# Pooled attention and a tanh-shrink MLP on one core: output stores moved to ScalarE's queue, q cast and turned by token blocks, pair sums one pair sooner

## The chip, the cores and the metric

The kernel runs on one core of a Trainium2 chip. The core has a matrix engine (TensorE, PE in the profile, PEld for its weight loads), VectorE (DVE), ScalarE (ACT), GpSimd (POOL), and SyncE (SP), which here only issues transfers. Transfers run on 16 DMA engines; SyncE and ScalarE each have a queue from which they issue them. The metric is the time of one execution in microseconds (us), lower is better.

## The reference, cut to what matters

Attention over keys and values that are averaged in groups of 8 rows, for 8 batches, 8 heads, 576 tokens and a head size of 64; its output, 4608 tokens by 512, goes through a two-layer MLP with 2048 hidden units.

```python
k_p = k.reshape(B, H, Sp, 8, D).mean(axis=3)          # Sp = 72
v_p = v.reshape(B, H, Sp, 8, D).mean(axis=3)
scores = scale * np.matmul(q, k_p.transpose(0, 1, 3, 2))
attn = np.exp(scores - scores.max(-1, keepdims=True))
attn = attn / (attn.sum(-1, keepdims=True) + 1e-9)
x = np.matmul(attn, v_p).transpose(0, 2, 1, 3).reshape(B * S, H * D)
h = x @ w_in                                           # 512 -> 2048
out = (h - np.tanh(h)) @ w_out                         # 2048 -> 512
```

## The kernel before, in words

The MLP works on groups of 512 tokens, nine of them (`g` = 0 to 8), the attention on batches of 576. Batch `nb = g + 1` is attended to while group `g` is in the MLP, and the inputs of batch `nn = g + 2` are loaded meanwhile. Group 0 has code of its own; the change is in the loop over groups 1 to 8, and "group" below means one turn of it.

A group has two stages. In the first, **h stage**, TensorE makes `h` in eight pairs of hidden blocks (`h_pair`, matmuls on L529, 8 per pair; the last pair as two halves, `h_one`). For each pair ScalarE takes the tanh (L541, L546), and VectorE subtracts it from `h` in PSUM and writes `Gt` in bf16 (L542, L547). `sum_p` (L550) adds the two members of finished pairs into `P`, two pairs in one instruction.

In the second stage the output product is done in seven smaller ones instead of eight, by Strassen's scheme: `product` (L585) multiplies `Gt`, `P`, `Q` or `Dg` with stored sums of the weights, in two halves of four pairs each, and `after_product` combines the seven in SBUF into `O`, which holds four tiles of 128 tokens by 512. The first product reads `Gt`, the second and third `P`. Between the half products TensorE does the scores of the next batch (L348), which need the turned q (`qT`), and, from the seventh on, attention times v (L395), whose result is turned by DMA into `xT` (L433), the next groups' MLP input.

q of the next batch comes from DRAM into `q_raw` (one buffer), is cast to bf16 by ScalarE into `q_bf` (`q_cast_part`, L192: two casts of four heads each, all four token blocks; L197: the 64 tokens left over), and turned by five DMA transposes (`q_dma_transpose`, L203). The three casts are issued before the tanhs of the first three pairs (pairs 1 to 3 in group 1), the five transposes after the last cast. The pooled k is turned likewise (L331) at the first pair. Right after the q transposes SyncE issues the nine loads of batch `nn`: k in two (L137, L146), v in five (L137, four times L141), q in two (L170, L162).

The results are stored by SyncE (`store`, L602): the upper two tiles of `O` (`store(g, 1)`) after the thirteenth half product, the lower two (`store(g, 0)`) at the group's end. Tokens are dealt over partitions in an interleaved order, so that a tile's rows are one or two stretches of the output, each with a transfer of its own.

Each engine's instructions run in the order in which the kernel states them[...]. Between engines the framework puts in the waits, and it deals completion counters to the transfers after a planner has lined up the engines' instructions by estimated time.

Of the kernel before, what the change touches and what calls it, by code (L numbers as in the profile page):

```python
# [9 lines left out]
BF16 = mybir.dt.bfloat16  # L10
# [5 lines left out]
B, H, S, D = 8, 8, 576, 64  # L16
POOL = 8
G = S // POOL
DM, DFF = 512, 2048
NHP = H // 2  # L20
R = 4
# [5 lines left out]
TG = 512  # L27
# [8 lines left out]
HT = TG // 2  # L36
# [6 lines left out]
def kernel(  # L43
# [9 lines left out]
    nc = tc.nc  # L53
# [5 lines left out]
    work = ctx.enter_context(tc.tile_pool(name="work", bufs=2))  # L59
# [44 lines left out]
    O = const.tile([128, 4, DM], FP32, name="O")  # L104
# [9 lines left out]
    q_bf = const.tile([128, R + 1, H, D], BF16, name="q_bf")  # L114
# [35 lines left out]
    def load_k(b):  # L150
        return [
            load_main(k_pairs, k_raw[b % 2], b, 0, NM),
            load_dense(k_pairs, k_raw[b % 2], b),
        ]

    def load_v(b):
        return [load_main(v_pairs, v_raw[b % 2], b, 0, NM)] + load_left(
            v_pairs, v_raw[b % 2], b
        )
# [6 lines left out]
    def load_q(b, tail=True):  # L166
        if b not in q_raws:
            q_raws[b] = raw.tile([128, H, R + 1, D], FP32, name="q_raw", tag="q_raw")
        t = q_raws[b]
        nc.sync.dma_start(  # L170
            out=t[:, :, 0:R, :], in_=q[b, :, 0:QA, :].rearrange("h (p j) d -> p h j d", j=R)
        )
        if tail:
            load_q_tail(b, t, nc.sync)

    qTs = {}
# [12 lines left out]
    def q_cast_part(b, n):  # L189
        t = q_raws[b]  # L190
        if n < 2:
            nc.scalar.copy(  # L192
                out=q_bf[:, 0:R, 4 * n : 4 * n + 4, :].rearrange("p j h d -> p h j d"),
                in_=t[:, 4 * n : 4 * n + 4, 0:R, :],
            )
        else:
            nc.scalar.copy(out=q_bf[:QT, R, :, :], in_=q_raws.pop(b)[:QT, :, R, :])  # L197

    def q_dma_transpose(b):
        qT = work.tile([128, NHP, S], BF16, name="qT", tag="qT")  # L200
        for j in range(R + 1):
            rows = 128 if j < R else QT
            nc.sync.dma_start_transpose(  # L203
                out=qT[:, :, j * 128 : j * 128 + rows],
                in_=q_bf[:rows, j, :, :].rearrange("p h d -> p (h d)"),
            )
        qTs[b] = qT

    def q_pe_transpose(b, hps, eng=None):
        if b not in qTs:  # L210
# [86 lines left out]
    def kb_main(kb, ps, t0, t1, engs):  # L297
        kv = kb.rearrange("p (t x) -> p t x", x=KP)
        engs[0](out=kv[0:D, t0:t1, 0:G], in_=ps[0:D, :, 0:G])
        engs[1](out=kv[D:128, t0:t1, G:128], in_=ps[D:128, :, G:128])  # L300

    def kb_left(kb, ps, eng):
        eng(
            out=kb[D:128, :].rearrange("p (t x) -> p t x", x=KP)[:, :, 128 : 128 + LO],
            in_=ps[D:128, 0 : NM * LO].rearrange("p (x t) -> p t x", t=NM),
        )
# [22 lines left out]
    def k_dma_transpose(b):  # L329
        kT = work.tile([128, NT, 128], BF16, name="kT", tag="kT", bufs=1)  # L330
        nc.sync.dma_start_transpose(  # L331
            out=kT[:, :, :], in_=kdups.pop(b)[:, :, :, :].rearrange("p t a d -> p (t a d)")
        )
        kTs[b] = kT

    def k_place(b, eng):
        kT = kTs.pop(b)
        kb_main(KB[b % 2], kT[:, 0:NM, :], 0, NM, (eng, eng))
        kb_left(KB[b % 2], kT[:, NM, :], eng)
# [115 lines left out]
    def out_segments(c0, nrows):  # L455
        segs = []
        r = 0
        while r < nrows:
            c = c0 + r
            bb = c // S  # L460
            i = c % S
            if i < QA:
                j = i // 128
                p0 = i % 128
                ln = min(128 - p0, nrows - r, QA - i)
                dst = out[bb * S : bb * S + QA, :].rearrange("(p j) m -> p j m", j=R)[
                    p0 : p0 + ln, j, :
                ]
            else:
                ln = min(S - i, nrows - r)  # L470
                dst = out[bb * S + i : bb * S + i + ln, :]
            segs.append((r, r + ln, dst))
            r += ln
        return segs
# [62 lines left out]
    def h_pair(g, p, b0, ts):  # L537
        h_mms(g, p, PS[:, b0, :])
        h_mms(g, p + NP, PS[:, b0 + 1, :])
        t2 = TS[:, 2 * ts : 2 * ts + 2, :]  # L540
        nc.scalar.activation(out=t2, in_=PS[:, b0 : b0 + 2, :], func=ACT.Tanh)  # L541
        nc.vector.tensor_sub(out=Gt[:, p, :, :], in0=PS[:, b0 : b0 + 2, :], in1=t2)  # L542

    def h_one(g, p, s, b0, ts):
        h_mms(g, p + s * NP, PS[:, b0, :])
        nc.scalar.activation(out=TS[:, ts, :], in_=PS[:, b0, :], func=ACT.Tanh)  # L546
        nc.vector.tensor_sub(out=Gt[:, p, s, :], in0=PS[:, b0, :], in1=TS[:, ts, :])  # L547

    def sum_p(a, b):
        nc.vector.tensor_tensor(  # L550
            out=P[:, a:b, :], in0=Gt[:, a:b, 0, :], in1=Gt[:, a:b, 1, :], op=ALU.add
        )

    def sum_q(a, b):
        nc.vector.tensor_tensor(
            out=Q[:, a:b, :], in0=Gt[:, a:b, 0, 0:HT], in1=Gt[:, a:b, 1, HT:TG], op=ALU.add
        )
# [9 lines left out]
    def w_sum(out, a, b, op, eng=nc.vector, k0=0, k1=NP):  # L567
        return eng.tensor_tensor(  # L568
            out=out[:, k0:k1, :], in0=a[:, k0:k1, :], in1=b[:, k0:k1, :], op=op
        )  # L570
# [23 lines left out]
    def chain(g, bk):  # L594
        if g == NG - 1 and bk == C1:
            return PS[:, 2:4, 0:HD]
        return PS[:, bk, :].rearrange("p (t n) -> p t n", t=2)

    def store(g, th, tts=(0, 1), c0=0, c1=DM):
        for tt in tts:  # L600
            for n, (r0, r1, dst) in enumerate(out_segments(g * TG + th * HT + tt * 128, 128)):
                nc.sync.dma_start(out=dst[:, c0:c1], in_=O[r0:r1, 2 * th + tt, c0:c1])  # L602

    def sh(c, off):
        return slice(c.start + off, c.stop + off)
# [99 lines left out]
    for m, base, step, cm in (  # L705
# [6 lines left out]
            out=m,  # L712
            in_=m,
# [6 lines left out]
    for i in range(2):  # L720
# [4 lines left out]
        out=spread.rearrange("p (t x) -> p t x", x=32)[:, :, 0:LO],  # L725
        in_=ident[:, 0 : NM * LO].rearrange("p (x t) -> p t x", t=NM),
# [156 lines left out]
    for u in range(16):  # L883
        qd, tb = u // 4, u % 4
# [27 lines left out]
        if u in (9, 11):  # L912
            n = (u - 9) // 2
            nc.scalar.mul(
                out=w2s[:, 4, 4 * n : 4 * n + 4, :], in_=b22[:, 4 * n : 4 * n + 4, :], mul=-1.0
# [10 lines left out]
    for g in range(1, NG):  # L926
        nb = g + 1 if g + 1 < B else None
        nn = g + 2 if g + 2 < B else None
        for p in range(NP - 1):
            c = p if g > 1 else p - 1  # L930
            if nb is not None and 0 <= c < 3:
                q_cast_part(nb, c)
            h_pair(g, p, (0, 2, 4, 6, 0, 2, 4)[p], p % 2)
            if g == 1 and p < 4:
                w_sum(w2s[:, 0, :, :], b11, b22, ALU.add, k0=2 * p, k1=2 * p + 2)
            if p >= 4:
                sum_p(2 * p - 8, 2 * p - 6)
            if nb is not None and p == 0:
                k_dma_transpose(nb)
                k_place(nb, nc.gpsimd.tensor_copy)  # L940
            if nb is not None and c == 2:
                q_dma_transpose(nb)
                if nn is not None:
                    load_k(nn)
                    load_v(nn)
                    load_q(nn)
        h_one(g, NP - 1, 1, 0, 2)
        h_one(g, NP - 1, 0, 1, 3)
        sum_p(6, 8)
        sum_q(0, 4)  # L950
        sum_q(4, 8)
        ps_a = Banks(2, 3, 4, 5, 0, 1)
        for u in range(14):
            n, half = u // 2, u % 2
            bk, lhs, rhs = products[n]
            if n == 6 and g == NG - 1:
                break
            product(g, bk, lhs, rhs, 4 * half, 4 * half + 4, n < 2)
            if half:
                after_product(g, n)  # L960
                if g == 1 and n in (1, 2):
                    w_sum(w2s[:, 2, :, :], b21, b22, ALU.add, k0=4 * n - 4, k1=4 * n)
            if nb is not None:
                if u < NT:
                    scores(nb, u)
                if u in (6, 7, 8, 9, 11):
                    av(nb, (6, 7, 8, 9, 11).index(u), ps_b1, True)
                if u == 6 and nn is not None:
                    pool_k(nn, nc.gpsimd)
                    pool_v(nn, nc.gpsimd)  # L970
            if u == 12:
                store(g, 1)
        if g < NG - 1:
            nc.scalar.copy(out=O[:, 0:2, 0:HD], in_=chain(g, C1))  # L974
            store(g, 0)
    store(NG - 1, 1)
    store(NG - 1, 0, c0=HD)
    bk, lhs, rhs = products[6]
# [40 lines left out]
```

## Time and profile before

Time before: 308.95 us, the median of 3 runs (308.21 to 310.93). The profiled execution has a span of 306.2 us at a mean granted TensorE clock of 0.989.

| view | what | us |
|---|---|---|
| busy | TensorE matmuls | 282.6 (92%) |
| busy | VectorE | 230.3 (75%) |
| busy | ScalarE | 154.1 (50%) |
| group | L529 h stage, 512 matmuls of 379 ns | 111.8 |
| group | L541 tanh of a pair, 56 of 1024 ns | 57.3 |
| group | L542 subtraction of a pair, 56 of 1221 ns | 68.4 |
| group | L550 pair sums, 32 of 683 ns | 21.8 |
| group | L192 casts of q, 12 of 1042 ns | 12.5 |
| SyncE's queue | L602 stores, 52 of 594 ns (median) | to landing 2.4 |
| SyncE's queue | L203 q transposes, 30 of 1257 ns (median) | to landing 2.5 |

Busy time is what an engine spent on instructions, not what it adds to the end. In the list of waits a line names who waited, for whom, the us in all, how often, and the longest. In a timeline a line gives the start, the length of a run of like instructions, the engine (SPq: SyncE's queue, where the length is that of issuing, not of the transfer), the line of code, and in brackets the idle time before it with what ended it.

### The profile page before, as it was taken

How to read it: one execution, taken by the hardware profiler on the slowest of the kernel's cores; microseconds unless marked ns; L12 is line 12 of the kernel's file. 1: busy time of each engine (PE TensorE's matmuls, PEld its weight loads, DVE VectorE, ACT ScalarE, POOL GpSimd, SP SyncE). 2: the span in 40 equal slices, each digit the busy share in tenths (PEclk: the TensorE clock that was granted, in tenths of full speed). 3: DMA queues.
4: the chain of work that ended last, by engine and by line, in shares of the span. 5: the costliest groups of instructions: out<-in, count | busy, mean ns of one | idle time of the engine just before them, and what ended most of it. 6: DMA issues, size and time to landing. Idle time of an engine off the chain costs nothing.

```text
span 306.2 us, 5451 instructions
## 1 busy us (share of the span) xinstructions
PE 282.6 (92%) x2040; PEld 179.3 (59%) x2040; DVE 230.3 (75%) x400; ACT 154.1 (50%) x244; POOL 121.3 (40%) x122
## 2 busy tenths in 40 slices
PE   7999899998989599999999978999998999999990
PEld 3554356446944388458745863479447945864780
DVE  5658577799968759598869883899687948937960
ACT  4657576676256352765275525660865056136320
POOL 8500819940793019802961296109910100100010
PEclk9999999999999899999999999999999999999997
DMA  7999999939637598749974997499560360040005
GB/s 260 217 222 276 314 243 296 205 77 322 161 62 176 116 334 134 193 77 347 174 167 98 333 157 186 91 323 186 118 146 2 64 153 2 0 131 8 0 9 130
DMA packets 66378, 49.84 MB, mean 163 GB/s; under 512 B 39984, under 2 KB 53296, under 8 KB 66352
## 3 DMA queue, kind: packets, MB, share of 16 engines
q1 hardware_dynamic: 59024, 42.94, 56.8%
q0 software_dynamic: 4752, 4.72, 9.2%
q10 hardware_dynamic: 2576, 1.84, 2.2%
q8 instruction: 16, 0.26, 0.4%
q14 instruction: 10, 0.08, 0.1%
HBM read 36.70 MB, written 9.44 MB: 151 GB/s over the span
## 4 chain that ended last, share of the span: by engine, by line
PE 60%; DMA 15%; DVE 12%; POOL 4%; ACT 3%; issue 3%; SPq 2%; ACTq 0%; POOLq 0%; DVEq 0%
PE PS L585 25%; PE PS L529 23%; DVE Gt L542 6%; DMA w1b<-in_moe_w_in_dram 4%; DMA qT<-q_bf 4%; PE PS L511 4%; DMA k_raw<-in_k_dram 4%; PE PS L348 3%; PE PS L395 3%; DMA xT<-x_sb 3%; DVE P L550 2%; ACT TS L541 2%; DVE w2s L568 1%; POOL k_raw L247 1%; SPq L203 1%
## 5 line engine op out<-in xcount | busy, mean ns | idle before, releaser
L529 PE MATMUL PS<-xT,w1b 128*128 128x512 bf16 x512 | 111.8, 379 | 4.7 <-DMA xT<-x_sb 3.8
L542 DVE TENSOR_TENSOR Gt<-PS,TS 128x1024 bf16<-128x1024 f32 x56 | 68.4, 1221 | 33.2 <-ACT TS L541 33.2
L529 PEld LDWEIGHTS <-w1b 128*128 128x128 f16 x512 | 49.8, 98 | 64.2 <-issue 3.7
L541 ACT ACTIVATE TS<-PS 128x1024 f32<-128x1024 f32 x56 | 57.3, 1024 | 35.0 <-PE PS L529 27.7
L626 POOL TENSOR_TENSOR m<-O,m 128x512 f32<-128x512 f32 x8 | 10.5, 1312 | 127.1 <-ACT m L625 65.5
L413 DVE TENSOR_TENSOR x_sb<-PS,rden 128x256 bf16<-128x256 f32 x72 | 30.5, 424 | 2.5
L585 PE MATMUL PS<-w2s,Dg 128*128 128x256 f16 x256 | 30.2, 273 | 0.0
L585 PEld LDWEIGHTS <-Gt 128*128 128x128 bf16 x256 | 24.8, 99 | 8.8 <-DVE Gt L547 2.7
L367 ACT ACTIVATE E<-PS 128x288 bf16<-128x288 f32 x60 | 21.8, 410 | 13.9 <-PE PS L348 13.7
L247 POOL TENSOR_TENSOR k_raw<-k_raw 128x512 f32<-128x512 f32 (+2 forms) x13 | 21.6, 1679 | 16.8 <-DMA k_raw<-in_k_dram 16.8
L585 PEld LDWEIGHTS <-P 128*128 128x128 bf16 x256 | 24.8, 99 | 5.0 <-issue 1.4
L585 PEld LDWEIGHTS <-Dg 128*128 128x128 bf16 x256 | 24.6, 98 | 2.7
L348 PE MATMUL PS<-qT,KB 128*128 128x288 bf16 (+5 forms) x128 | 18.1, 293 | 5.9 <-DMA qT<-q_bf 5.7
L560 DVE TENSOR_TENSOR Dg<-Gt 128x1024 bf16<-128x1024 bf16 x32 | 22.1, 750 | 0.0
L550 DVE TENSOR_TENSOR P<-Gt 128x1024 bf16<-128x1024 bf16 x32 | 21.8, 683 | 0.3
L395 PE MATMUL PS<-VB,E 128*128 128x130 bf16 x240 | 20.2, 220 | 0.1
L632 ACT COPY m<-PS 128x512 f32<-128x512 f32 x8 | 4.7, 585 | 29.5 <-PE PS L585 29.5
L585 PE MATMUL PS<-w2s,Gt 128*128 128x256 f16 x128 | 18.0, 282 | 1.6 <-DVE Gt L547 1.5
L266 POOL TENSOR_TENSOR v_raw<-v_raw 128x512 f32<-128x512 f32 (+1 forms) x12 | 19.2, 1620 | 0.0
L395 PEld LDWEIGHTS <-E 128*128 128x128 bf16 x240 | 16.8, 98 | 1.9 <-issue 0.4
L585 PE MATMUL PS<-w2b,P 128*128 128x256 f16 x128 | 16.6, 276 | 0.0
L974 ACT COPY O<-PS 128x512 f32<-128x512 f32 x7 | 4.1, 586 | 24.6 <-PE PS L585 24.6
(108 smaller groups left out, 386.0 us busy)
## 6 DMA issues: line engine op xcount, KB each, us to landing
k_raw<-in_k_dram SPq DMA_DIRECT2D x7, 1024.0 KB, 5.8
q_raw<-in_q_dram SPq DMA_DIRECT2D x7, 1024.0 KB, 10.2
v_raw<-in_v_dram SPq DMA_DIRECT2D x7, 1024.0 KB, 8.4
out_dram<-O SPq DMA_DIRECT2D x36, 128.0 KB, 2.4
out_dram<-O SPq DMA_DIRECT2D x16, 256.0 KB, 2.7
w1b<-in_moe_w_in_dram POOLq DMA_DIRECT2D x4, 512.0 KB, 13.9
w2b<-in_moe_w_out_dram POOLq DMA_DIRECT2D x4, 512.0 KB, 17.0
k_raw<-in_k_dram SPq DMA_DIRECT2D x7, 128.0 KB, 6.0
```

The lines of the kernel that those rows point to most:

```text
L247: first = eng.tensor_tensor(out=r[:, ta:tb, 0:4, :], in0=r[:, ta:tb, 0:4, :], in1=r[:, ta:tb, 4:8, :], op=ALU.add)
L266: eng.tensor_tensor(out=r[:, ta:tb, 0:4, :], in0=r[:, ta:tb, 0:4, :], in1=r[:, ta:tb, 4:8, :], op=ALU.add)
L348: nc.tensor.matmul(dst[p : p + w], lhsT=KB[b % 2][:, o : o + w], rhs=qTs[b][:, m, c0:c1], start=True, stop=True,)
L367: nc.scalar.activation(out=E[:, t, half * hs : (half + 1) * hs], in_=ps[:, :], func=ACT.Exp, scale=SCALE)
L395: nc.tensor.matmul(ps[:, 2 * n : 2 * n + 2, :].rearrange("p h d -> p (h d)") if n < 2 else ps.rearrange("p (a s) d -> p a s d", s=2)[:, :, ...
L413: nc.vector.tensor_tensor(out=x_sb[:, half, :, :], in0=ps[:, :, 0:D], in1=rden[:, :, :].to_broadcast([128, 4, D]), op=ALU.mult,)
L529: nc.tensor.matmul(dst, lhsT=w1b[:, fb, i * 128 : (i + 1) * 128], rhs=xT[:, fb, c0 : c0 + TG], start=(fb == 0), stop=(fb == NFB - 1),)
L541: nc.scalar.activation(out=t2, in_=PS[:, b0 : b0 + 2, :], func=ACT.Tanh)
L542: nc.vector.tensor_sub(out=Gt[:, p, :, :], in0=PS[:, b0 : b0 + 2, :], in1=t2)
L550: nc.vector.tensor_tensor(out=P[:, a:b, :], in0=Gt[:, a:b, 0, :], in1=Gt[:, a:b, 1, :], op=ALU.add)
L560: nc.vector.tensor_tensor(out=Dg[:, a:b, :, :], in0=Gt[:, a:b, :, 0:HT], in1=Gt[:, a:b, :, HT:TG], op=ALU.subtract,)
L585: nc.tensor.matmul(part(g, bk, tt), lhsT=lhs(k, slice(tt * 128, (tt + 1) * 128)), rhs=rhs[:, k, :], start=(first and k == 0 and (tt == 0 o ...
```

## The change

Four edits. The stores of a finished group leave SyncE's queue: for groups 1 to 7 `store_tile` issues each of the four tiles from ScalarE in the next group's h stage, after the tanhs of pairs 3 to 6. (Group 0 and the last group store as before.) The two large casts of q take two token blocks of all heads each instead of all blocks of four heads, and the q transposes follow in three parts, each after the cast that it needs. The sums into `P` are issued after pairs 3, 4 and 5 instead of 4, 5 and 6. The aim is a shorter queue on SyncE ahead of the transposes and loads, and sums that are ready sooner.

```diff
     def q_cast_part(b, n):
...
-                out=q_bf[:, 0:R, 4 * n : 4 * n + 4, :].rearrange("p j h d -> p h j d"),
-                in_=t[:, 4 * n : 4 * n + 4, 0:R, :],
+                out=q_bf[:, 2 * n : 2 * n + 2, :, :].rearrange("p j h d -> p h j d"),
+                in_=t[:, :, 2 * n : 2 * n + 2, :],
...
-    def q_dma_transpose(b):
-        qT = work.tile([128, NHP, S], BF16, name="qT", tag="qT")
-        for j in range(R + 1):
+    def q_dma_transpose(b, j0=0, j1=R + 1):
+        if j0 == 0:
+            qTs[b] = work.tile([128, NHP, S], BF16, name="qT", tag="qT")
+        qT = qTs[b]
+        for j in range(j0, j1):
...
+    def store_tile(g, tb):
+        for r0, r1, dst in out_segments(g * TG + tb * 128, 128):
+            nc.scalar.dma_start(out=dst, in_=O[r0:r1, tb, :])
...
-            if p >= 4:
-                sum_p(2 * p - 8, 2 * p - 6)
+            if 3 <= p < 6:
+                sum_p(2 * p - 6, 2 * p - 4)
+            if g > 1 and p >= 3:
+                store_tile(g - 1, p - 3)
             if nb is not None and p == 0:
                 k_dma_transpose(nb)
                 k_place(nb, nc.gpsimd.tensor_copy)
+            if nb is not None and 0 <= c < 3:
+                q_dma_transpose(nb, 2 * c, min(2 * c + 2, R + 1))
             if nb is not None and c == 2:
-                q_dma_transpose(nb)
                 if nn is not None:
                     load_k(nn)
...
-            if u == 12:
-                store(g, 1)
         if g < NG - 1:
             nc.scalar.copy(out=O[:, 0:2, 0:HD], in_=chain(g, C1))
-            store(g, 0)
```

More of the change, by code (lines that the diff above doesn't have):

```diff
@@ L206, in q_dma_transpose @@
             )
-        qTs[b] = qT
     def q_pe_transpose(b, hps, eng=None):
@@ L597, in chain, with store @@
         return PS[:, bk, :].rearrange("p (t n) -> p t n", t=2)
-    def store(g, th, tts=(0, 1), c0=0, c1=DM):
-        for tt in tts:
-            for n, (r0, r1, dst) in enumerate(out_segments(g * TG + th * HT + tt * 128, 128)):
+    def store(g, th, c0=0, c1=DM):
+        for tt in range(2):
+            for r0, r1, dst in out_segments(g * TG + th * HT + tt * 128, 128):
                 nc.sync.dma_start(out=dst[:, c0:c1], in_=O[r0:r1, 2 * th + tt, c0:c1])
+    def store_tile(g, tb):
+        for r0, r1, dst in out_segments(g * TG + tb * 128, 128):
+            nc.scalar.dma_start(out=dst, in_=O[r0:r1, tb, :])
     def sh(c, off):
```

## The prediction

> **What bounds the kernel now.** I read the page's busy shares first, then who waited for whom, then TensorE's and SyncE's timelines group by group.
>
> ```profile
> PE 282.6 (92%) x2040; PEld 179.3 (59%) x2040; DVE 230.3 (75%) x400; ACT 154.1 (50%) x244; POOL 121.3 (40%) x122
> ```
>
> TensorE is busy 92%; only its idle 23.6 us and work that other engines put into its path can be won. The list of waits says which idle time the change can reach:
>
> ```profile
> PE PS L348 <- DMA qT<-q_bf: 5.7, 5, 2.6
> PE PS L529 <- DMA xT<-x_sb: 3.8, 2, 3.0
> PE PS L585 <- DVE Gt L547: 1.5, 3, 0.8
> ```
>
> The columns are us in all, times, longest. TensorE's timeline shows two of them at their largest, in group 2 and at the start of group 5:
>
> ```profile
> 100.78 1.04 PE L585 MATMUL PS<-w2s,Gt 128*128 128x256 f16 x8
> 102.50 0.28 PE L348 MATMUL PS<-qT,KB 128*128 128x288 bf16 x1 [0.67 <-DMA qT<-q_bf]
> 105.36 0.40 PE L348 MATMUL PS<-qT,KB 128*128 128x288 bf16 x1 [2.58 <-DMA qT<-q_bf]
> 184.72 13.97 PE L529 MATMUL PS<-xT,w1b 128*128 128x512 bf16 x64 [2.95 <-DMA xT<-x_sb]
> ```
>
> The starts of L529 give the groups: 55.53 (group 1), 86.96, 121.27, 151.51, 184.72, 214.20, 244.91, 271.45. Group 5 (29.48 us) is nearly free of waits. Against it group 2 (34.31) loses 4.8, group 4 (33.21) 3.7, group 1 (31.43) 2.0, group 6 (30.71) 1.2, group 3 (30.24) 0.8.
>
> Why qT is late is in SyncE's queue (group 3; issue start, length):
>
> ```profile
> 123.93 2.94 SPq L602 DMA_DIRECT2D out_dram<-O  x5
> 126.97 1.26 SPq L331 DMA_TRANSPOSE kT<-kd  x1
> 128.34 7.22 SPq L203 DMA_TRANSPOSE qT<-q_bf  x5
> 135.60 0.58 SPq L137 DMA_DIRECT2D k_raw<-in_k_dram  x1
> 139.52 0.42 SPq L170 DMA_DIRECT2D q_raw<-in_q_dram  x1
> 141.19 0.67 SPq L162 DMA_DIRECT2D q_raw<-in_q_dram  x1
> ```
>
> Everything goes one after another: stores, kT, five qT, loads. The last qT is issued near 134.4, the scores want it at 136.0.
>
> **What decides what the change costs** is one more wait, and the transfers' landing times:
>
> ```profile
> SPq L162 <- DMA k_raw<-in_k_dram: 8.5, 6, 1.9
> k_raw<-in_k_dram SPq DMA_DIRECT2D x7, 1024.0 KB, 5.8
> v_raw<-in_v_dram SPq DMA_DIRECT2D x7, 1024.0 KB, 8.4
> out_dram<-O SPq DMA_DIRECT2D x36, 128.0 KB, 2.4
> ```
>
> L162 (q's tail) reads and writes nothing of k_raw, yet waits for that load, which is eight transfers ahead of it (k, k rest, v, four v rests, q, then q tail). The framework deals eight completion counters in turn to all transfers of SyncE and ScalarE, in the order in which its planner lines them up, and a transfer isn't issued until the previous holder of its counter has landed. ScalarE's stores will draw from the same eight.
>
> [...] a store costs SyncE 0.59 us (L602), ScalarE 0.53 (L988). [...] The trace agrees for SyncE (L433's wait held its queue up to 9.4 us); for ScalarE no run here shows a long one.
>
> **The change, part by part.**
>
> 1. *Stores leave SyncE.* Groups 2 to 6 lose 8, 5, 7, 6, 6 stores, 0.59 us each: SyncE reaches kT 3 to 6.4 us sooner. In group 3 (start S = 121.27) kT goes at S+2.7, five qT of 1.27 us follow, the last goes at S+9.1 and lands 2.5 later, S+11.6. Scores start at S+14.7. So the qT waits go: 3.25 + 0.46 + 0.70 + 1.32 = 5.7 us. Loads start at S+10.3, where they started at S+14.3.
>
> 2. *Cast and turn by blocks.* The casts keep their size (128x1024, 1.04 us each, tail 0.61), so ScalarE's time is the same. The first two turns need cast 0 alone; without it SyncE would stand until the tail cast ends at S+5.4. Counted in part 1. The rows read become 512 B runs out of the same tile; I take no cost.
>
> 3. *Sums one pair sooner.* VectorE does 1.13 to 1.22 us per pair and 0.60 to 0.68 per sum at a pace of 1.73 us per pair, so three sums leave it slightly behind. Moved to pairs 3 to 5, the fourth pair's idle 0.5 us takes one, and the last subtractions (L547) come 0.6 us sooner. That removes L547's waits: 0.81 in group 1, about 0.45 in groups 7 and 8 each (0.33 beside a late pair), 0.26 in group 5: 2.0 us.
>
> 4. *Stores on ScalarE, if none waits.* 44 issues of 0.53 to 0.62 us. A pair of tanhs takes 1.02 of 1.73 us, and the issue runs beside the tanh (in the trace ScalarE's issues at 13.31 began while the exp of 13.25 ran). Two stores, 1.2 us, fit into a pair. Cost nothing: the 0.70 us in which ScalarE waits for L529 hides it.
>
> 5. *Stores on ScalarE that wait.* Behind a waiting store stand the tanhs of pairs 6 and 7, then VectorE's L542 and L547, then product 0. So I count places. In groups 2 to 5 the order is kT, five qT, k, k rest, v, ..., with stores of pair 3 and on between them. The last qT stands at place 6, k at 7, so any store at place 15 or later waits for a load. Stores before the last: 7, 4, 6, 5 in groups 2, 3, 4, 5. How many loads the planner puts ahead of the last store isn't in the trace. Bounds: one (k alone, ready at pair 2's tail cast) and all nine. I take four or five: after a 1 MB load about two pairs of tanhs pass in the planned order, so k goes before pair 3, v about pair 4, the first v rests about pairs 5 and 6. Then the last store stands eight places behind v in groups 2 and 4, behind k rest in groups 3 and 5.
>
>    k goes at S+10.3, k rest at S+10.9 and lands 6.0 later, S+16.9; v at S+11.5 and lands 7.7 later (group 3's own value; 10.1 in group 4), S+19.2. After that 0.6 issue, 0.6 tanh, 0.68 L547, 0.2 for the last two matmuls: product 0 ends at S+19.0 (k rest) or S+21.3 (v), where free it ends at S+15.8. Lost 3.2 or 5.5 us.
>
> **The sum**, change against before: group 1 -0.8; group 2 +5.5-4.5 = +1.0; group 3 +3.2-0.6 = +2.6; group 4 +5.5-0.9 = +4.6; group 5 +3.2-0.3 = +2.9; group 6 -1.3; groups 7 and 8 -0.9. In group 4 TensorE comes later while q's load is issued about as before (SyncE's v rests now wait for k), so the 2.95 us xT wait at 184.72 is absorbed: -2.9. In all +5.2 us: 314.1. I shade it by 1 us, as one or two of these places may fall on a landed transfer: **313.0 us**.
>
> **The rivals.**
>
> *A: no store waits long.* For it: only loads are slow (5.8 to 10 us); stores and turns land in 2.5. Against it: loads now move into the very pairs in which the stores stand. Then parts 1 and 3 are won, -5.7 - 2.0, and the xT wait at 184.72 shrinks since loads end 4 us sooner, -1 to -2.9. That gives 308.95 - 8.7 to 10.6, about 299.5 us.
>
> *B: half of it.* Groups 3 and 5 have the fewest stores; if only groups 2 and 4 meet a load, +2.6 and +2.9 become -0.6 and -0.3: 314.1 - 6.4 = 307.7. If in group 2 the last store also falls on a landed one (+1.0 becomes -4.5), 302.
>
> *C: worse.* Two stores in a row wait, v lands in 10.1 us as in group 4, SyncE's loads wait in their turn and xT transposes stand behind them. Some 2.4 us more in groups 2 and 4 and one xT wait of 3: about 321.
>
> *D: ScalarE is the bound even without waits*, since 44 issues of 0.55 are 24 us. Against it: 27.7 us of L541's idle time waited for TensorE. At worst 0.5 us in six groups: 303.
>
> **The numbers.** Forecast (stores wait for loads in most groups) 0.48, A with D 0.27, B 0.17, C 0.08. The limits of 1% are 305.9 and 312.0. Faster: A, D and half of B, 0.36. Slower: C and three quarters of the forecast, 0.44. Same: the rest, 0.20. The range leaves out the best of A and most of C: 299 to 319.
>
> **What would show it.** Right: no qT wait in groups 2 to 6, ScalarE's queue waiting for k_raw or v_raw at the store's line, TensorE idle before the first product of groups 2 to 5 on L542 or L547, with gaps of 3 to 5 us. Each step alone: kT issued about 2.6 us after a group's start; loads about 10.3 after it. Wrong: ScalarE's tanhs at an even 1.73 us to the end of each group while stores lie among them, and a first product without a gap; then A holds, and part 5 is the step that failed.

## The result, and the profile after

The changed kernel takes 326.93 us, the median of 4 runs (325.92 to 327.75), against 308.58 (304.35 to 310.93, now of 4 runs) before it: a ratio of 1.067, with an interval of 1.054 to 1.081. (This ratio, like all below, is of fast executions alone, without those over 1.5% above the fastest of the same kernel, so it can differ from that of the medians.) By the medians it is slower by 18 us, where 4 were predicted (5.2 before the shading) and 319 was the top of the range. The profiled execution has a span of 324.4 us (306.2 before) at a mean clock of 0.963 (0.989).

The page of the changed kernel, the row of TensorE's busy time and the row of its granted clock in 40 slices of the span:

```profile
PE 287.1 (88%) x2021; PEld 181.2 (56%) x2040; DVE 229.6 (71%) x400; ACT 153.0 (47%) x244; POOL 122.7 (38%) x122
PEclk9999999999999589999999699998999999999998
```

TensorE's idle time went from 23.6 to 37.3 us, and its busy time grew by 4.5 us though its work is the same (the trace lacks the records of 19 matmuls: x2021 in place of x2040). Both are to be explained; the 5 and 8, the 6, and the 8 after it in the clock row lie in the middle of groups 2, 4 and 5 and are the second part. Its list of waits for the first part:

```profile
PE PS L586 <- DVE Gt L543: 15.6, 5, 5.8
PE PS L586 <- DVE Gt L548: 4.6, 4, 2.9
PE PS L530 <- DVE x_sb L414: 2.5, 2, 1.8
PE PS L530 <- DMA xT<-x_sb: 0.9, 1, 0.9
```

(L586 is the product, L585 before; L530 the h stage, L529 before; L543 and L548 the subtractions, L542 and L547 the tanhs, L607 the store on ScalarE; in the variants below the numbers can shift by one or two more.) The qT waits, 5.7 us before, are gone. In their place product 0 waits 20.2 us for the last `Gt`. ScalarE's list of waits says why those are late:

```profile
ACT TS L542 <- DMA k_raw<-in_k_dram: 10.1, 2, 5.7
ACT TS L542 <- DMA out_dram<-O: 5.2, 1, 5.2
ACT TS L547 <- DMA out_dram<-O: 1.8, 1, 1.8
```

A tanh reads nothing of k, and nothing that a store writes. ScalarE's timeline in group 2 shows what stands between (ACTq: issuing on ScalarE):

```profile
98.53 1.17 ACTq L607 DMA_DIRECT2D out_dram<-O  x2
99.80 1.02 ACT L542 ACTIVATE TS<-PS 128x1024 f32<-128x1024 f32 x1 [2.78 <-PE PS L530]
105.25 1.12 ACTq L607 DMA_DIRECT2D out_dram<-O  x2
106.48 1.02 ACT L542 ACTIVATE TS<-PS 128x1024 f32<-128x1024 f32 x1 [5.65 <-DMA k_raw<-in_k_dram]
106.50 2.73 ACTq L607 DMA_DIRECT2D out_dram<-O  x2
109.34 1.08 ACT L547 ACTIVATE TS<-PS 128x512 f32<-128x512 f32 x2 [1.83 <-DMA out_dram<-O]
```

The two stores of pair 5 could go beside the tanh, at about 99.8. They go at 105.25 and 105.77. The built program deals them the counters of the two loads of k, which SyncE issued at 98.83 and 99.45, and which landed at 105.23 and 105.74. The tanh of pair 6 stands behind them. Of the stores of pair 6 the first goes at once; the second goes at 108.71, and the last tanhs stand behind it. Its counter is that of the first rest of v (L141):

```profile
98.83 0.57 SPq L137 DMA_DIRECT2D k_raw<-in_k_dram  x1
100.81 8.02 SPq L141 DMA_DIRECT2D v_raw<-in_v_dram  x4
DMA to landing us min/median/max: 7.9/7.9/7.9
```

The last line is the landing time of the first of these four: issued at 100.81, it landed at 108.69. The list of waits puts this wait, and the 5.2 us, down to a store (out_dram<-O), but the landing times say otherwise. Where a store of groups 2 to 5 was dealt the counter of another store, that one had landed 3.2 us or more before. The 5.2 us lie in group 4, where two stores are issued at 175.37 and 179.21, just after the loads of k (175.35) and of v (179.18) have landed. So loads make all of the long waits. Stores of pair 4 wait too, up to 2.8 us, for turns of q; in group 3 nothing else is of note. TensorE over the stretch in group 2:

```profile
102.38 0.60 PE L586 MATMUL PS<-w2s,Gt 128*128 128x256 f16 x4
108.81 0.61 PE L586 MATMUL PS<-w2s,Gt 128*128 128x256 f16 x2 [5.84 <-DVE Gt L543]
110.72 0.61 PE L586 MATMUL PS<-w2s,Gt 128*128 128x256 f16 x2 [1.29 <-DVE Gt L548]
111.59 1.92 PE L586 MATMUL PS<-w2b,P 128*128 128x256 f16 x8
113.78 1.91 PE L586 MATMUL PS<-w2b,P 128*128 128x256 f16 x8
117.51 1.05 PE L586 MATMUL PS<-w2s,P 128*128 128x256 f16 x8
```

7.1 us of gap, and then the cost that the prediction has no term for: eight matmuls take 1.92 us where they take 1.05 a little later. The windows of the changed kernel (columns: us, then busy us and count of PE, PEld, DVE, ACT, POOL, then the granted clock, share of DMA, GB/s) show it in the clock:

```profile
107.00:109.00 2.00, 0.18 (x1) 0.13 (x2) 1.23 (x1) 0.50 (x1) 0.00 (x0) 0.50 0.91 326
113.00:115.00 2.00, 2.00 (x11) 1.39 (x10) 0.19 (x1) 0.71 (x2) 0.00 (x0) 0.50 0.84 253
117.00:119.00 2.00, 2.00 (x24) 1.47 (x23) 1.89 (x4) 1.12 (x3) 0.00 (x0) 1.00 0.00 0
```

A full window of 2 us at clock 0.50 does 11 matmuls, at 1.00 it does 24. The clock is halved already during the gap, and it stays so until about 116.4, as the 0.65 of the window from 115 to 117 says: 5.7 us after the gap's end at 110.7.

By group, from TensorE's start to the next group's start (predicted: the sum of the prediction, with its 2.9 us for the xT wait in group 4, where that wait lies):

| group | before | after | measured | predicted | gap in product 0 | TensorE busy, before and after |
|---|---|---|---|---|---|---|
| 1 | 31.43 | 31.69 | +0.3 | -0.8 | 0.16 + 0.20 | 29.77, 29.84 |
| 2 | 34.31 | 39.95 | +5.6 | +1.0 | 5.84 + 1.29 | 31.05, 32.60 |
| 3 | 30.24 | 31.48 | +1.2 | +2.6 | 0.85 + 0.21 | 29.56, 29.63 |
| 4 | 33.21 | 40.18 | +7.0 | +1.7 | 4.17 + 2.94 | 29.55, 31.20 |
| 5 | 29.48 | 35.72 | +6.2 | +2.9 | 4.59 | 29.39, 31.03 |
| 6 | 30.71 | 29.21 | -1.5 | -1.3 | 0 | |
| 7 and 8 | 61.3 | 60.7 | -0.6 | -0.9 | 0 | |
| sum | | | +18.2 | +5.2 | 19.9 in groups 2 to 5 (17.4 predicted) | |

### The profile page after: what moved, and what is told of

It reads as the page before. It is cut to its first block, busy times and chain, and to the rows that moved or that the text cites. A ratio compares the mean times of both kernels' runs of the same rounds, so it can differ in the third digit from the quotient of the medians.

```text
span 324.4 us, 5421 instructions
## 1 busy us (share of the span) xinstructions
PE 287.1 (88%) x2021; PEld 181.2 (56%) x2040; DVE 229.6 (71%) x400; ACT 153.0 (47%) x244; POOL 122.7 (38%) x122
## 4 chain that ended last, share of the span: by engine, by line
PE 57%; DMA 17%; DVE 10%; POOL 4%; SPq 3%; ACT 3%; issue 2%; ACTq 1%; DVEq 0%; POOLq 0%
PE PS L586 26%; PE PS L530 21%; DMA k_raw<-in_k_dram 7%; DMA w1b<-in_moe_w_in_dram 4%; DVE Gt L543 4%; PE PS L512 3%; PE PS L396 3%; PE PS L349 3%; DMA v_raw<-in_v_dram 3%; SPq L205 3%; ACT TS L542 2%; DMA qT<-q_bf 2%; DVE x_sb L414 1%; DVE w2s L569 1%; POOL k_raw L248 1%
## 5 line engine op out<-in xcount | busy, mean ns | idle before, releaser
L530 PE MATMUL PS<-xT,w1b 128*128 128x512 bf16 x496 | 111.1, 379 | 5.4 <-DVE x_sb L414 2.5
L543 DVE TENSOR_TENSOR Gt<-PS,TS 128x1024 bf16<-128x1024 f32 x56 | 68.4, 1222 | 46.9 <-ACT TS L542 46.9
L530 PEld LDWEIGHTS <-w1b 128*128 128x128 f16 x512 | 49.7, 98 | 64.2 <-issue 2.8
L542 ACT ACTIVATE TS<-PS 128x1024 f32<-128x1024 f32 x56 | 57.3, 1025 | 53.5 <-PE PS L530 26.6
L631 POOL TENSOR_TENSOR m<-O,m 128x512 f32<-128x512 f32 x8 | 11.5, 1438 | 159.9 <-ACT m L630 125.6
L586 PEld LDWEIGHTS <-Gt 128*128 128x128 bf16 x256 | 23.9, 98 | 28.3 <-DVE Gt L543 17.0
L586 PE MATMUL PS<-w2s,Gt 128*128 128x256 f16 x128 | 19.4, 286 | 20.2 <-DVE Gt L543 15.6
L586 PE MATMUL PS<-w2s,Dg 128*128 128x256 f16 x256 | 30.2, 272 | 0.0
L586 PEld LDWEIGHTS <-P 128*128 128x128 bf16 x256 | 26.4, 105 | 6.7 <-issue 1.4
L248 POOL TENSOR_TENSOR k_raw<-k_raw 128x512 f32<-128x512 f32 (+2 forms) x13 | 22.5, 1746 | 16.3 <-DMA k_raw<-in_k_dram 16.3
L586 PEld LDWEIGHTS <-Dg 128*128 128x128 bf16 x256 | 24.6, 98 | 2.8 <-issue 0.2
L561 DVE TENSOR_TENSOR Dg<-Gt 128x1024 bf16<-128x1024 bf16 x32 | 23.2, 785 | 0.0
L396 PE MATMUL PS<-VB,E 128*128 128x130 bf16 x240 | 20.2, 220 | 0.1
L586 PE MATMUL PS<-w2b,P 128*128 128x256 f16 x128 | 19.8, 310 | 0.0
L267 POOL TENSOR_TENSOR v_raw<-v_raw 128x512 f32<-128x512 f32 (+1 forms) x12 | 19.2, 1623 | 0.0
L586 PE MATMUL PS<-w2s,P 128*128 128x256 f16 x128 | 16.5, 275 | 0.0
```

What stands on the lines that cost most here:

```text
L248: first = eng.tensor_tensor(out=r[:, ta:tb, 0:4, :], in0=r[:, ta:tb, 0:4, :], in1=r[:, ta:tb, 4:8, :], op=ALU.add)
L267: eng.tensor_tensor(out=r[:, ta:tb, 0:4, :], in0=r[:, ta:tb, 0:4, :], in1=r[:, ta:tb, 4:8, :], op=ALU.add)
L396: nc.tensor.matmul(ps[:, 2 * n : 2 * n + 2, :].rearrange("p h d -> p (h d)") if n < 2 else ps.rearrange("p (a s) d -> p a s d", s=2)[:, :, ...
L530: nc.tensor.matmul(dst, lhsT=w1b[:, fb, i * 128 : (i + 1) * 128], rhs=xT[:, fb, c0 : c0 + TG], start=(fb == 0), stop=(fb == NFB - 1),)
L561: nc.vector.tensor_tensor(out=Dg[:, a:b, :, :], in0=Gt[:, a:b, :, 0:HT], in1=Gt[:, a:b, :, HT:TG], op=ALU.subtract,)
L586: nc.tensor.matmul(part(g, bk, tt), lhsT=lhs(k, slice(tt * 128, (tt + 1) * 128)), rhs=rhs[:, k, :], start=(first and k == 0 and (tt == 0 o ...
```

## The experiments

All ratios are against the kernel before, run on the same chip. Theory W is the prediction's: stores on ScalarE wait for a completion counter that a slow transfer still holds. Theory I is its rival: issuing 44 stores on ScalarE, or their traffic beside the turns, is itself what delays the tanhs. A second rival was that the loads, which the change starts sooner, do harm by themselves.

**The change without its stores, and the stores without the rest of the change.** The first undoes the new place of the stores and keeps the casts by blocks and the earlier sums; the second puts only this into the kernel before:

```diff
...
+            if g > 1 and p >= 3:
+                store_tile(g - 1, p - 3)
...
-            if u == 12:
-                store(g, 1)
...
-            store(g, 0)
```

> The change without its stores part: stores on SyncE as before, casts and turns by blocks, sums one pair sooner. Both theories: the turns still stand behind the stores, so the qT waits stay, only the waits for L547 go: 306 to 309 us. If casts by blocks (512 B runs) cost, or turns in three parts do, above 310 us.

> The kernel before with only the stores moved to ScalarE; casts by heads, all turns after the last cast, sums after pairs 4 to 6. Theory W: the turns start some 3 us later than in the change, so do the loads, and the waiting stores hold the tanhs as long or longer: 325 to 332 us. Theory I: as the change, about 327 us. If instead casts or sums were what costs, it would lie near 300 to 309 us.

Without the new place of the stores: 305.91 us, ratio 0.998 (0.995 to 1.001). The stores alone: 326.99 us, ratio 1.065 (1.057 to 1.072). The whole loss is the stores' part; the rest of the change neither makes it nor is needed for it. With the stores alone, ScalarE waits in the same way (two of the lines of its list of waits):

```profile
ACT TS L541 <- DMA out_dram<-O: 6.3, 2, 5.5
ACT TS L541 <- DMA k_raw<-in_k_dram: 4.0, 1, 4.0
```

(The 5.5 us that the list puts down to a store are again a load of k: it landed at 174.68, and the store was issued at 174.70.)

**Loads held back.** The changed kernel, with the loads of the next batch stated after the tanh of the last pair's first half and the first of them made to wait for it, so that no store can be dealt a counter behind a load still on its way:

```diff
-                if nn is not None:
-                    load_k(nn)
-                    load_v(nn)
-                    load_q(nn)
+                pass
-        h_one(g, NP - 1, 1, 0, 2)
+        th7 = h_one(g, NP - 1, 1, 0, 2)
+        if nn is not None:
+            after(load_k(nn)[0:1], th7)
+            load_v(nn)
+            load_q(nn)
```

> The changed kernel with one wait added: the next batch's k load (and so the loads behind it) waits for the tanh of block 7a, so that every ScalarE store gets its counter ahead of the loads and none stands behind a k or v load. Theory W (stores wait for loads through the shared counters, the tanhs behind them starve TensorE, whose clock then drops): gaps before the first product of groups 2 to 5 gone, 298 to 303 us. Theory I (issuing 44 stores on ScalarE, or their traffic beside the turns, is itself what delays the tanhs): little changes, 318 to 327 us.

302.84 us, ratio 0.986 (0.979 to 0.992). All 44 stores are on ScalarE, at the same places, and no product waits for `Gt` any more; what TensorE waits for is now xT:

```profile
PE PS L530 <- DMA xT<-x_sb: 5.4, 3, 2.4
```

So issuing from ScalarE costs nothing that shows in itself, against theory I; the waits for the counters, with what follows from them, cost the difference of the two kernels, 24 us.

**Held back in group 4 alone.** The same edit with `g == 4` as its condition.

> The change with the loads held back to the tanh of block 7a in group 4 alone. Theory W: in group 4 no store is dealt a counter that a load holds, so its gap before the second half of the first product (7.1 us in the change) is gone, and with it the low clock there; groups 2 and 5 keep theirs. 6 to 9 us less than the change, 318 to 321 us. Theory I: group 4 keeps its gap.

A single run: 313.22 us, less than expected. Group 4 falls from 40.18 to 31.75 us and its gap is gone; group 2 keeps its gaps (5.07 + 1.87). So far the theory holds group by group. But group 5 fell as well, from 35.72 to 32.84 (gap 1.38 in place of 4.59), which was not expected. Its counters are dealt as before; only its timing moved. The load of k landed 15.8 us after the group's start in place of 17.4, and TensorE's h stage took 15.7 us in place of 14.0, in one run of matmuls behind an xT wait of 2.37 us (at half clock for part of it, as an estimate from these two times). The two together are 3.3 us, about what the gap lost.

**Stores left out.** The stores of groups 1 to 7 aren't done at all, once with the change's casts and turns by blocks, once with the old ones.

> The changed kernel with the stores of groups 1 to 7 left out (their part of the output is not written). Loads start about 10 us after a group's start as in the change. Theory W: no ScalarE wait, no gap before the first product: 296 to 301 us, close to the kernel with the loads held back (302.8). If loads that come this early did harm by themselves (traffic beside the turns), above 305 us.

> The kernel with the stores of groups 1 to 7 left out, with casts by heads and all five turns after the last cast, as before the change. The first turn then waits for the tail cast, 5.4 us into the group, the last lands 14.3 us after its start, where the scores want it at 14.7: 296 to 298 us against 295.9, so the casts part is worth 0 to 2 us once the stores are out of SyncE's queue.

295.91 us (ratio 0.964, 0.960 to 0.968) and 296.05 us (0.963, 0.958 to 0.967). With loads as early as in the change and no stores, every group from 2 to 6 takes 29.2 us, and the only wait of TensorE there that reaches half a microsecond is 0.9 us for xT just before the first of them. That fells the second rival: early loads do no harm. It also says that the casts by blocks are worth nothing once the queue is free, and it sets the bound for what any place of the stores can reach.

**Stores early in the group.** After the tanhs of pairs 0 and 1 instead of 3 to 6, where by my reckoning eight places back there were only transfers that land in 2.5 us.

```diff
-            if g > 1 and p >= 3:
-                store_tile(g - 1, p - 3)
+            if g > 1 and p < 2:
+                for tb in ((2, 3), (0, 1))[p]:
+                    store_tile(g - 1, tb)
```

> The changed kernel with the stores after the tanhs of pairs 0 and 1 (two tiles each) instead of pairs 3 to 6; loads where the change has them, about 10 us after a group's start. All stores get their counters ahead of the loads. Theory W: no wait for a load, at most a short one for a q turn at pair 1 (2 to 3 us, early in the stage, where TensorE has pairs in hand): 299 to 305 us. Theory I: as many issues in fewer pairs, 318 us or more.

317.26 us, ratio 1.032 (1.026 to 1.038): the expectation was wrong. ScalarE's list of waits, and then TensorE's:

```profile
ACT q_bf L197 <- DMA out_dram<-O: 8.4, 2, 4.7
ACT q_bf L192 <- DMA out_dram<-O: 6.8, 3, 2.7
```

```profile
PE PS L530 <- DVE Gt L543: 14.2, 11, 3.3
```

No load is met, and no store either, though the list puts most of it down to stores: each store that goes late goes within 0.1 us of the landing of a turn of q, k or x (at 130.53, for one, after a turn of q at 130.51). It is q's casts and the first tanhs that stand behind. A short landing was no safety here (the casts waited up to 4.7 us): what counted is that the instruction behind the store was needed at once.

**Half and half.** The upper two tiles back on SyncE, the lower two on ScalarE after pairs 3 and 4:

```diff
-            if g > 1 and p >= 3:
+            if g > 1 and 3 <= p < 5:
                 store_tile(g - 1, p - 3)
...
+            if u == 12:
+                store(g, 1)
```

> A version meant to beat both: the upper two tiles stored by SyncE after the thirteenth half product, as before the change, the lower two by ScalarE after pairs 3 and 4 only; the rest as in the change. With two to four ScalarE stores the last one is dealt its counter at most seven places behind k's load, so none waits for a load; SyncE's queue is 1 to 2.4 us longer, the last turn lands about 14 us into the group, the scores want it at 14.7. Theory W: no gap in groups 2 to 5, 297 to 302 us, ratio 0.965 to 0.985. Theory I: half the issues, half the loss, 312 to 318 us.

307.16 us, ratio 0.998 (0.995 to 1.000): missed too. The load waits are gone, but now stores meet counters of q's turns:

```profile
ACT TS L542 <- DMA qT<-q_bf: 7.4, 2, 4.3
```

**Stores on GpSimd.** In the built program GpSimd's transfers have completion counters of their own. Same stores at the same places (`nc.gpsimd.dma_start` for `nc.scalar.dma_start` in `store_tile`), and a second form with all of a group's stores at the next group's start, ahead of GpSimd's work on k, and `pool_v` moved behind that.

> The changed kernel with the same stores at the same place issued by GpSimd, whose transfers have counters of their own. Theory W: neither the stores nor the loads wait for each other, gaps gone, GpSimd has the time (busy 40%): 296 to 303 us. Theory I (issues or traffic beside the turns): traffic is as in the change, 315 us or more.

> A version meant to beat both: stores on GpSimd (counters of their own) at the start of the next group, ahead of k_place and of pool_v, which moves from the group before to behind k_place; casts, turns and sums as in the change. The stores' traffic ends before the turns of q, the loads start about 10 us after a group's start and meet no store. Theory W: 296 to 300 us, ratio 0.96 to 0.98, below the stores on GpSimd at pairs 3 to 6 (302.1). If stores beside xT and kT turns cost as much as beside the q turns: 301 to 305 us.

302.05 us, ratio 0.981 (0.975 to 0.987), and 302.82 us, 0.984 (0.980 to 0.988); the second was expected at 296 to 300. Against theory I, the long gaps before the product are gone in both, though the same stores are moved. In the first form, whose profile is of the slowest of its four executions (304.16), TensorE's waits are the old ones, in part:

```profile
PE PS L530 <- DMA xT<-x_sb: 4.5, 3, 3.2
PE PS L349 <- DMA qT<-q_bf: 3.4, 3, 1.6
```

The second form removes most of these (qT none, xT 1.4), has small waits for `Gt` again (2.1 in all), and is no faster by its median; what holds it there was not tried. Together with the held loads these are the versions with all stores that beat both kernels, by 1.4 to 1.9%; their intervals overlap, so none is shown to be the best.

**The sums one pair sooner, alone,** in the kernel before.

> The kernel before with the pair sums one pair sooner and nothing else. The waits for L547 go (0.8, 0.3 and 0.3 us in groups 1, 7, 8 and 0.3 in group 5), in groups 2 to 4 and 6 the qT waits hide it: ratio 0.993 to 0.998.

Ratio 0.993 (0.990 to 0.996), which is about -2.1 us, the size predicted. But the medians of all executions, 306.85 against 307.55, are only 0.7 us apart, and the change without its stores, which has these sums too, gave 0.998 (0.995 to 1.001) on another chip. Between nothing and 3 us; the runs don't settle it closer.

**A ladder of gaps.** Is the halved clock a matter of the gap itself, or of the transfers around it? In the kernel without stores, 4, 7, 10, 13 and 17 extra tanhs on a tile of their own stand ahead of the last pair's tanhs in groups 2 to 6. TensorE then waits in product 0 for ScalarE's plain work, and for no transfer.

> As the kernel with the stores left out, and ahead of the tanh of block 7a stand 4, 7, 10, 13, 17 idle tanhs (0.6 us each) in groups 2, 3, 4, 5, 6: gaps of TensorE of about 1.5, 3, 5, 7, 9 us made without any transfer. If the low clock after a gap is TensorE's own (theory W's second term), a stretch at half clock follows the gaps of 3 us and more, 3 to 8 us long; if it came from the transfers or from ScalarE's queue, the clock stays at 1.0 after these gaps.

A single run: 332.16 us. Two of the five gaps in TensorE's timeline, and windows after all five (columns as above):

```profile
104.36 0.39 PE L587 MATMUL PS<-w2s,Gt 128*128 128x256 f16 x2 [1.33 <-DVE Gt L549]
173.44 0.61 PE L587 MATMUL PS<-w2s,Gt 128*128 128x256 f16 x2 [5.31 <-DVE Gt L549]
```

```profile
104.30:108.00 3.70, 3.64 (x32) 3.05 (x32) 3.40 (x7) 2.98 (x9) 0.00 (x0) 1.00 1.05 318
137.00:140.50 3.50, 3.42 (x20) 2.51 (x21) 2.52 (x5) 2.30 (x7) 0.00 (x0) 0.65 1.09 315
173.40:176.00 2.60, 2.56 (x12) 1.80 (x13) 2.48 (x4) 1.55 (x5) 0.00 (x0) 0.50 1.12 309
176.00:179.00 3.00, 3.00 (x16) 2.06 (x14) 0.47 (x1) 1.01 (x3) 0.00 (x0) 0.50 0.05 5
179.00:182.00 3.00, 3.00 (x33) 2.30 (x32) 2.63 (x5) 1.71 (x5) 0.00 (x0) 0.99 0.00 0
212.80:216.00 3.20, 3.15 (x15) 2.18 (x16) 2.48 (x4) 1.64 (x6) 0.00 (x0) 0.50 0.10 20
253.90:257.00 3.10, 3.01 (x14) 2.11 (x15) 2.52 (x5) 1.60 (x5) 0.00 (x0) 0.50 0.00 0
```

After 1.33 us of gap the clock is full. After 3.32 us it is 0.65 over 3.5 us, after 5.31 it is 0.50 for 5.6 us, after 7.29 and 9.94 it is 0.50 for about 3.7 and 3.6. At half clock a stretch of 3.5 to 5.6 us does half of its work: 1.7 to 2.8 us are lost behind each gap. No transfer is needed for it: behind the fifth gap the DMA share is 0.00 and the clock 0.50, behind the first it is 1.05 and the clock 1.00. Of these gaps a longer one doesn't cost more of it. The times agree: this run is 36 us above the kernel without stores (295.91), and its gaps add up to 27.2 us; the rest, 9 us, is about what the low clock takes.

## Why the prediction was wrong

**Part 1, stores leave SyncE: right.** The qT waits are gone. SyncE's timeline in group 3 (which starts at 127.11):

```profile
129.82 1.23 SPq L332 DMA_TRANSPOSE kT<-kd  x1
131.16 7.56 SPq L205 DMA_TRANSPOSE qT<-q_bf  x5
138.77 0.58 SPq L137 DMA_DIRECT2D k_raw<-in_k_dram  x1
```

kT goes 2.7 us after the start, as predicted; the loads at 11.7, 1.4 later than predicted, as the turns take 7.56 us in place of five times 1.27. In the changed kernel this gain is buried under the new waits; the kernel without stores shows what it is worth.

**Part 2, casts by blocks at no cost: right** (295.91 against 296.05). **Part 3, -2.0: not settled,** as above. In the changed kernel group 1 gained nothing: of the 0.81 us, 0.36 stayed, and 0.54 turned up in the h stage, on L543.

**Part 4, issues on ScalarE cost nothing: right.** With the loads held back, 44 issues lie among the tanhs and no product waits as much as 0.3 us. Rival D falls with it.

**Part 5, the mechanism: right, and shown.** Rival A (no store waits long) and B (half of it) fall by ScalarE's list of waits and the landing times; removing the load that holds the counter removes the gap. Where it was off is which store meets what. In the built program three stores are dealt counters behind loads in group 2, two in group 4, one in group 5 and none in group 3, because the planner put more of SyncE's loads ahead of ScalarE's stores in some groups than in others. So group 3 lost 1.1 us and not 3.2, where stores met only turns of q. Group 5 lost 4.6 and not 3.2: a store of pair 5 waited, with two pairs of tanhs still behind it. Groups 2 and 4 lost 7.1 and not 5.5: two stores waited one after the other, as rival C had it, for k and then for a part of v, which landed 21.5 and 20.6 us after the group's start, where the prediction has 19.2. The sum of these, 17.4, came out as 19.9: wrong in its parts, 2.5 short in all.

**The sum: this is the step that failed.** It puts down a loss in product 0 as the length of the gap. The prediction is 13.0 us short of the measured +18.2 before its shading. The terms, from the table and the waits:

- 6.6 us is TensorE at half clock after the gaps, for which the sum has no term. Against 29.4 us of busy time in a group without gaps, groups 2, 4 and 5 have 32.60, 31.20 and 31.03: 3.2 + 1.8 + 1.6. In group 2 the profile before already had 1.65 us of it (31.05 busy; eight matmuls at 105.55 took 1.92 us behind the 2.58 us wait that the prediction quotes), and the prediction took that as won with the qT wait, without asking what the new and longer gaps would cost of the same kind.
- 2.5 us are the gaps, as above.
- 2.4 us: the xT wait at the end of group 4 was not absorbed. It went from 2.95 to 1.76, waiting for x_sb now, not to nothing; and a wait of 0.69 on x_sb came at the end of group 3. Probably the attention comes later because its scores stand in the same queue of TensorE as the products that were held up; no run isolates it.
- 1.1 us: group 1, where the gain of 0.8 didn't come and the group is 0.3 longer.

Together 12.6 of 13.0; the first is half of it. The shading by 1 us, for places that fall on a landed transfer, did not pay: the last stores of groups 3, 4 and 5 did fall on one, but stores ahead of them waited. Rival C, "worse" (about 321 us), came nearest and named the second waits, but it too priced no clock.

**What the trace of before left open** is whether ScalarE's queue, too, stands still behind an issue that waits. In the changed kernel it does: tanhs stood idle for 5.7 and 5.2 us behind stores that waited for loads of k.

## What to carry to other kernels

Here the stores that moved to the queue of a computing engine brought their waits for a free counter with them, and the tanhs that the engine had to do next stood behind them, for up to 5.7 us. So count, in the order of the built program, what the counter's previous holder is and when that lands, or take an engine whose next work is not urgent. Before pricing an idle stretch of TensorE in the middle of its work, look at the clock behind a like gap in the profile at hand: here gaps of 3.32 to 9.94 us before a product cost 1.6 to 3.2 us on top of their length. A change that only moves transfers is best tested with the transfers left out: that run told at once what could be won at most (12 us) and that nothing else was wrong. And where a list of waits names a transfer, compare the time of the issue that waited with the landing times: here the list named stores, and it was loads.

## What the runs showed of the hardware that was not expected

Whether the clock was halved after a gap did not go by the gap's length alone. In the kernel with held loads two xT waits at a group's start came out the other way round (the windows' columns as above):

```profile
118.85 2.38 PE L530 MATMUL PS<-xT,w1b 128*128 128x512 bf16 x5 [1.97 <-DMA xT<-x_sb]
182.53 1.67 PE L530 MATMUL PS<-xT,w1b 128*128 128x512 bf16 x6 [2.43 <-DMA xT<-x_sb]
```

```profile
118.85:122.00 3.15, 3.06 (x8) 1.22 (x10) 0.00 (x0) 0.00 (x0) 2.99 (x3) 0.56 0.39 74
182.50:185.50 3.00, 2.92 (x13) 1.39 (x15) 0.00 (x0) 1.00 (x2) 2.83 (x3) 1.00 0.48 89
```

In the 3.15 us after 1.97 us of waiting the clock was 0.56, in the 3 us after 2.43 us it was 1.00. The kernel before has a like pair: behind the wait of 2.58 us in group 2, with 0.67 us just ahead of it, and behind its longest, 2.95 us at 184.72:

```profile
106.00:107.00 1.00, 1.00 (x6) 0.74 (x5) 0.00 (x0) 0.20 (x1) 0.00 (x0) 0.50 0.91 268
184.70:186.00 1.30, 1.28 (x6) 0.60 (x7) 0.00 (x0) 0.00 (x0) 1.30 (x1) 1.00 0.53 99
```

Of these four waits those of 1.97 and 2.58 us cost clock, those of 2.43 and 2.95 us did not. What makes the difference was not shown.

A store issued by GpSimd took 0.54 us to issue (median, at pairs 3 to 6), against 0.59 from SyncE in the kernel before and 0.48 from ScalarE in the changed one, but 4.1 us to landing (median of the 128 KB stores, in both forms), against 2.4 from SyncE in the kernel before, 2.9 from ScalarE in the changed one and 2.5 with the loads held back.
